# A spectral mixing layer beside an MLP on one core: another hand-written order of the first two weight blocks, a shorter normalisation factor, and another order of a product's passes

## The chip, the core and the metric

The kernel runs on one core of a Trainium2 chip. The metric is the device time of one execution in microseconds (us); the kernel before has three runs. Beside them stands one profiled execution, whose trace is read below.

## What is computed

```python
# x: 2048 x 576; w1: 576 x 4608; w2: 4608 x 576; the DFT matrices are 2048 x 2048 and 576 x 576, real and imaginary part
xn = _layernorm(x)                        # (x - mean) / sqrt(var + 1e-5)
a, b = xn @ dft_hid_re.T, xn @ dft_hid_im.T
y = dft_seq_re @ a - dft_seq_im @ b       # real part of a transform over both axes
h = maximum(xn @ w1, 0)
return x + y + h @ w2
```

## The kernel before

Every fp32 operand is split into a high and a low half in fp16 (the high part by ScalarE, the low part, the difference to it, by VectorE or GpSimd), and each product takes three passes on TensorE: high by high, high by low, low by high. The 4608 columns of the MLP are taken in nine blocks of 512 (b), the 2048 tokens in four groups of 512 (g), each of four tiles of 128 (t = 4 g + c). From block 1 on the products are made of seven sums of quarters in place of eight quarters (`PRODUCTS`, `pair_products`), whose operands are sums of quarters too. After the blocks come the two transforms.

All work stands in an order written out by hand: strings of words (`BLOCK0`, `BLOCK1`, `BLOCK` for each of blocks 2 to 7, `BLOCK8`, `TURN`). `run` and `run_block` go through the words and issue what each names; every engine does its own instructions in exactly that order, and waits at an instruction until its operands are there. The words that the prediction follows, with the lines of the profile:

- `f:n` issues n matmuls of nothing (`fill`, L1072), which keep TensorE going until there is work.
- `bn`, `ag`, `sq`, `ch` make mean, variance and the factor of a tile (L471, L475, L480, L487 to L492). `hi` writes the high half of the normalised tile (L511, L514), `xn` the normalised tile itself (L531 on ScalarE, L533 on VectorE), `lo` the low half (L519, L520, on VectorE where the word ends in V, on GpSimd where it ends in G).
- `T` transposes a tile's halves into `xT` by DMA from SyncE's queue (L541). For tiles 0 and 1 `th` and `tl` do it on TensorE instead (L552), and `ch_`, `cl` copy the result on ScalarE (L1111, L1112).
- `lx`, `L1`, `L2` load x, w1 and w2 (L344; L360, L371, L372; L348), also from SyncE's queue. `pa` to `pd` and `na` to `nd` make the scales of w1 of blocks 0 and 1, `q` and `rm`, `w` those of w2, from the sums of `sw` and `rw` (L960). `wh`, `wl`, `nh`, `nl` split w1 into halves (L918; L923, L924), `uh`, `ul` split w2 (L1013, L1017).
- `p:t:i` and `p0:f` are block 0's first product for a single tile (L586), `P:g:f` that for a group at once, `oa` and `od` its result's halves (L601, L609), `m:g:k` the second product (L847), `e` its eviction, `ad` the addition to `spill` in DRAM.
- `ts` makes sums of the normalised tiles (L653), `tu` and `tv` their halves (L511, L514; L519, L520), `tw` their transposes by DMA (L660, L664). There are two buffers for these halves (`spare`), used by turns, so a `tu` waits for the `tw` two places ahead of it to land.
- In block 1 `p:t:i:k` is one of the seven products (L710), `f:t:i:k` its way out of the bank (L700 on ScalarE, L702 on VectorE); a word that begins with 0 is one of block 0 that stands among block 1's.

A product's matmuls take the weight planes of `w1s` (0 to 2 high, 3 and 4 low, 2 holds both remainders) and those of `xT` in the order of `PASSES`; for the first products (`p0`) `WK0` puts the high planes first.

Of the kernel before, what the change touches and what calls it, by code (L numbers as in the profile page):

```python
# [78 lines left out]
p:0:0:1 w:0:1 p:0:0:5 p:0:1:1 0tu:3:3 0ad:2:1 0ad:1:3 0tv:3:3:G f:0:0:1:V w:0:2 w:0:3 0tu:3:2
f:0:0:5:A f:0:1:1:A p:0:0:6 p:0:1:6 w:0:4 f:0:0:6:A p:0:0:7 p:0:0:3 0tv:3:2:G 0e:2:3:V f:0:0:7  # L80
# [1522 lines left out]
```

## Time and profile before

| | us |
|---|---|
| three runs: median (lowest to highest) | 1232.77 (1230.32 to 1237.54) |
| the profiled execution: its own time | 1230.08 |
| its span from first to last instruction | 1228.3 |
| TensorE busy in it, pieces and waits included as the page counts them | 1216.8 |
| granted clock of TensorE, mean over the span | 1.00 of full speed |

The profiled execution lies 0.24 us below the fastest of the three runs and 2.69 us below their median. 1.8 us of its time lies outside its span. The page has the busy time of each engine; TensorE is busy for 99% of the span, and every other engine has idle time. So in this table the time of the kernel is TensorE's work and the few places at which TensorE stands still.

### The profile page before, as it was taken

What the parts mean: (1) busy time and instruction counts of PE and PEld (TensorE: products, weight loads), DVE (VectorE), ACT (ScalarE), POOL (GpSimd) and SP (SyncE); (2) the same over time, 40 slices, a digit from 0 to 9 for tenths busy, and PEclk for the clock granted to TensorE, in tenths of its full rate; (3) what the DMA queues carried; (4) which work ended last, traced back from release to release, by engine and by line L of the source; (5) the groups of instructions that cost most, each with busy time, mean ns of one, the idle gap of its engine ahead of it and who ended that gap; (6) DMA issues with size and microseconds to landing.
All of it is one profiled execution on the core that took longest, in us unless ns stands there. A gap on an engine that the chain in (4) does not pass through costs nothing.

```text
span 1228.3 us, 26251 instructions
## 1 busy us (share of the span) xinstructions
PE 1216.8 (99%) x10514; PEld 1000.4 (81%) x10514; DVE 1059.0 (86%) x2052; ACT 724.2 (59%) x1258; POOL 210.7 (17%) x272
## 2 busy tenths in 40 slices
PE   9999999999999999999999999998999999999998
PEld 9867888888888888888888888876777777777777
DVE  8977999989898889888888889999877869987885
ACT  7855776766756667657667547666444445534342
POOL 3522122122122121221121111200211110000000
PEclk9999999999999999999999999999999999999999
DMA  8997478778778777776666678631755532255441
GB/s 240 205 178 179 142 157 189 150 152 155 161 146 169 149 145 169 138 145 147 154 117 142 142 180 168 115 95 41 200 128 137 130 81 48 89 159 180 143 132 35
DMA packets 127052, 175.98 MB, mean 143 GB/s; under 512 B 48337, under 2 KB 88785, under 8 KB 126929
## 3 DMA queue, kind: packets, MB, share of 16 engines
q1 hardware_dynamic: 97696, 121.99, 34.1%
q0 software_dynamic: 28672, 51.92, 29.7%
q8 instruction: 82, 1.34, 0.5%
q10 hardware_dynamic: 560, 0.39, 0.1%
q14 instruction: 42, 0.34, 0.1%
HBM read 112.53 MB, written 56.62 MB: 138 GB/s over the span
## 4 chain that ended last, share of the span: by engine, by line
PE 90%; DVE 6%; DMA 2%; ACT 1%; issue 1%; POOL 1%; SPq 0%; DVEq 0%; POOLq 0%
PE bank L710 26%; PE p L1476 26%; PE p L807 25%; PE pd L1390 7%; PE p L586 3%; PE p L847 3%; DMA raw_w<-in_w_dram 1%; DVE R L1363 1%; DMA xT<-dbuf 1%; DVE st L471 0%; DMA accs<-in_x_dram 0%; DMA accs<-wbuf 0%; DVE wbuf L923 0%; DVE cs L1017 0%; DVE tb L1403 0%
## 5 line engine op out<-in xcount | busy, mean ns | idle before, releaser
L807 PE MATMUL p<-w2s,h 128*128 128x288 f16 x2688 | 357.3, 286 | 0.0
L1476 PE MATMUL p<-R,cs 128*128 128x288 f16 x2688 | 331.0, 286 | 2.5 <-DVE cs L1017 2.5
L1476 PEld LDWEIGHTS <-cs 128*128 128x128 f16 x2688 | 262.8, 98 | 69.6 <-DVE cs L1017 3.4
L807 PEld LDWEIGHTS <-h 128*128 128x128 f16 x2688 | 263.0, 98 | 62.1 <-issue 0.2
L710 PEld LDWEIGHTS <-dbuf 128*128 128x128 f16 x1568 | 153.2, 98 | 21.9 <-issue 1.9
L710 PEld LDWEIGHTS <-wbuf 128*128 128x128 f16 x1568 | 153.4, 98 | 20.6 <-issue 0.3
L1013 ACT ACTIVATE cs<-tb,sc_c 128x1024 f16<-128x1024 f32 x56 | 64.1, 1148 | 82.8 <-PE p L1476 55.7
L710 PE MATMUL bank<-xT,dbuf 128*128 128x256 f16 x896 | 110.9, 273 | 0.0
L710 PE MATMUL bank<-xT,wbuf 128*128 128x256 f16 x896 | 110.5, 273 | 0.1
L1017 DVE SCALAR_TENSOR_TENSOR cs<-tb,sc_c,cs 128x1024 f16<-128x1024 f32 x56 | 71.7, 1283 | 22.8 <-ACT cs L1013 22.2
L710 PE MATMUL bank<-accs,dbuf 128*128 128x256 f16 x672 | 86.3, 273 | 1.4 <-ACT accs L700 0.8
L832 POOL DMA_DIRECT2D spill<-dbuf x70 | 61.0, 912 | 155.3 <-DVE dbuf L825 112.4
L710 PE MATMUL bank<-accs,wbuf 128*128 128x256 f16 x672 | 85.9, 273 | 0.0
L1013 ACT ACTIVATE cs<-accs,sc_c 128x1024 f16<-128x1024 f32 x40 | 45.9, 1147 | 58.5 <-PE p L1476 45.7
L757 DVE TENSOR_TENSOR h<-s,h 128x1024 f16<-128x1024 f32 x64 | 77.4, 1217 | 2.4 <-ACT h L751 2.4
L751 ACT ACTIVATE h<-s 128x1024 f16<-128x1024 f32 x64 | 66.5, 1049 | 10.8 <-DVE s L748 10.8
L719 ACT ACTIVATE h<-accs 128x256 f16<-128x256 f32 x128 | 51.1, 410 | 33.0 <-DVE accs L734 23.7
L1237 ACT ACTIVATE f<-f 128x1024 f32<-128x1024 f32 x64 | 67.1, 1049 | 4.5 <-DMA f<-in_cim_dram 3.4
L832 POOL DMA_DIRECT2D spill<-wbuf x42 | 39.5, 940 | 155.0 <-DVE wbuf L825 126.5
L1017 DVE SCALAR_TENSOR_TENSOR cs<-accs,sc_c,cs 128x1024 f16<-128x1024 f32 x40 | 51.2, 1282 | 13.7 <-ACT cs L1013 13.3
L700 ACT ACTIVATE accs<-bank 128x256 f32<-128x256 f32 x99 | 37.4, 380 | 39.2 <-PE bank L710 13.6
L821 ACT ACTIVATE dbuf<-p,c_ub 128x576 f32<-128x576 f32 x61 | 45.0, 737 | 24.0 <-PE p L807 24.0
(227 smaller groups left out, 1898.5 us busy)
## 6 DMA issues: line engine op xcount, KB each, us to landing
spill<-dbuf POOLq DMA_DIRECT2D x80, 288.0 KB, 4.6
f<-in_cre_dram SPq DMA_DIRECT2D x32, 512.0 KB, 4.8
...
```

The lines of the kernel that those rows point to most:

```text
L710: nc.tensor.matmul(ps, l, r, start=first and m == 0, stop=m == len(todo) - 1, skip_group_check=not first,)
L719: nc.scalar.activation(next(high_low(q)), SOURCE[q], AF.Relu)
L751: order["s"] = nc.scalar.activation(next(high_low(SUMS)), stage_of(slice(1, 5)), AF.Copy).ins
L757: order["lo"] = nc.vector.tensor_tensor(lo, stage_of(slice(1, 5)), hi, ALU.subtract).ins
L807: nc.tensor.matmul(ps[:, c], h[:, x, qa, c * P : (c + 1) * P], w[:, y, qb], start=first and i == 0 and j == 0, stop=i == NQ - 1 and j == 2 ...
L821: freed(nc.scalar.activation(o, ps, AF.Copy, scale=us[b]))
L832: nc.gpsimd.dma_start(spill[g, row, col], sums[g, row, col], accum_op=ALU.add)
L1013: nc.scalar.activation(hi, src, AF.Copy, scale=s)
L1017: nc.vector.scalar_tensor_tensor(lo, src, s, hi, ALU.mult, ALU.subtract)
L1237: nc.scalar.activation(f, f, AF.Abs, scale=2.0**-10, accum_out=sums_c[:, n, q : q + 1])
L1390: nc.tensor.matmul(ps, x[:, k, c * P : (c + 1) * P], dsp[z][:, a, y], start=first and m == 0, stop=m == len(PASSES) - 1, skip_group_check= ...
L1476: nc.tensor.matmul(ps, w[:, a, RANK[k]], r[:, c, RIGHT[rq]], start=first and k == 0 and j == 0, stop=k == HK - 1 and j == 2, skip_group_ch ...
```

## The change

Three things are changed. The words of blocks 0 and 1 are put in another order, in which some are given to another engine; no word is added or taken away, but the number after `f` sums to 235 where it was 240. The factor of the normalisation takes five steps on VectorE where it took six: `sq` scales the root by 1/8, and one Newton step of the root and two reciprocals give the factor. And `WK`, the order of a product's 14 passes in block 0, has the high planes of both operands first, then the low planes of x, the remainders, and last the low planes of the weights, for `p0`, `p` and `P` alike.

```diff
 SX = 4.0
+CX = 0.5 / SX
 EPS = 1e-5
...
-    nc.vector.memset(eps, EPS)
+    nc.vector.memset(eps, EPS * CX * CX)
...
     def deviation(a, b):
-        nc.scalar.activation(u[:, a : b + 1], mv[:, a : b + 1, 1], AF.Sqrt, bias=eps)
+        nc.scalar.activation(u[:, a : b + 1], mv[:, a : b + 1, 1], AF.Sqrt, bias=eps, scale=CX * CX)
     def factor(a, b):
...
         nc.vector.reciprocal(r0[:, c], u[:, c])
-        stt(u[:, c], v, EPS, r0[:, c], ALU.add, ALU.mult)
-        tt(u[:, c], u[:, c], r0[:, c], ALU.mult)
-        nc.vector.tensor_scalar(u[:, c], u[:, c], -0.5 * SX, 1.5 * SX, ALU.mult, ALU.add)
-        tt(r[:, c], u[:, c], r0[:, c], ALU.mult)
+        stt(r[:, c], v, EPS, r0[:, c], ALU.add, ALU.mult)
+        stt(u[:, c], r[:, c], CX * CX, u[:, c], ALU.mult, ALU.add)
+        nc.vector.reciprocal(r[:, c], u[:, c])
         stt(sh[:, c], m, -1.0, r[:, c], ALU.mult, ALU.mult)
...
-    WK0 = sorted(WK, key=lambda w: (0, 0, 1, 2, 2)[w[1]])
+    WK.sort(key=lambda w: (w[2] > 2, w[2] > 2, 2, 3, 3)[w[1]])
+    WK0 = WK
...
 BLOCK0 = """
-bn:0 ag:0 sq:0:0 ch:0:0 bn:1 ag:1 bn:2 bn:3 ag:2 ag:3 ms:0 hi:0 sq:1:3 mc:0 f:121 pa:0 ch:1:3
+bn:0 ag:0 sq:0:0 ch:0:0 bn:1 ms:0 hi:0 xn:0:A ag:1 mc:0 bn:2 f:92 pa:0 f:9 th:0 ch_:0 bn:3 pb:0
...
```

Of the words that name an engine, those of blocks 0 and 1 together stand so: `xn` 11 on ScalarE and 5 on VectorE before, 14 and 2 now; `lo` 10 on GpSimd and 6 on VectorE before, 9 and 7 now; `ts` 6 and 10 before, 7 and 9 now; `tv` 6 and 10 before, 8 and 8 now; `e` 21 on ScalarE and 5 on VectorE before, 22 and 4 now; `f` 23 and 1 before, 22 and 2 now.

The lines of the changed kernel are two higher than those of before from the constants on, and one higher between the factor and the order of passes. What the new order does to the engines is seen at three places.

**The transposes of the third token group, on SyncE's queue, at about 43 to 54 us of the trace.** `raw_w1_1_0` and `raw_w1_1_1` are block 1's two halves of w1, `xT2` holds the third token group. Before:

```order
L660 DMA_TRANSPOSE accs_98<-wbuf_97 128x10x128
L360 DMA raw_w1_1_0_1227<-in_w1_dram 128x4x256
L371 DMA raw_w1_1_0_1227<-in_w1_dram 96x2x128
L372 DMA raw_w1_1_0_1227<-in_w1_dram 32x2x128
L371 DMA raw_w1_1_0_1227<-in_w1_dram 96x2x128
L372 DMA raw_w1_1_0_1227<-in_w1_dram 32x2x128
L541 DMA_TRANSPOSE xT2_136<-dbuf_96 128x10x128 x4
L664 DMA_TRANSPOSE accs_98<-wbuf_97 128x5x128
L664 DMA_TRANSPOSE xT0_134<-wbuf_97 128x5x128
L664 DMA_TRANSPOSE accs_98<-wbuf_97 128x5x128
```
Now:

```order
L346 DMA x14_100<-in_x_dram 128x576
L362 DMA raw_w1_1_1_1200<-in_w1_dram 128x4x256
L373 DMA raw_w1_1_1_1200<-in_w1_dram 96x2x128
L374 DMA raw_w1_1_1_1200<-in_w1_dram 32x2x128
L373 DMA raw_w1_1_1_1200<-in_w1_dram 96x2x128
L374 DMA raw_w1_1_1_1200<-in_w1_dram 32x2x128
L362 DMA raw_w1_1_0_1206<-in_w1_dram 128x4x256
L373 DMA raw_w1_1_0_1206<-in_w1_dram 96x2x128
L374 DMA raw_w1_1_0_1206<-in_w1_dram 32x2x128
L373 DMA raw_w1_1_0_1206<-in_w1_dram 96x2x128
L374 DMA raw_w1_1_0_1206<-in_w1_dram 32x2x128
L542 DMA_TRANSPOSE xT2_136<-dbuf_96 128x10x128 x4
```
Both loads of block 1's w1 now stand ahead of the four transposes into `xT2`; before, one of them stood ahead and the other behind the four transposes (L664) that follow.

**The first tiles on ScalarE, from 10.6 us on.** L480 is a root, L511 and L514 a high half, L531 a normalised tile, L918 a high half of weights, L1111 and L1112 the copies `ch_:0` and `cl:0`. Before:

```order
L480 ACTIVATE u_142<-mv_140,eps_138 128x3
L511 ACTIVATE dbuf_96<-accs_98,sh_144,r_143 128x2x256
L514 ACTIVATE dbuf_96<-accs_98,sh_144,r_143 128x2x2x32
L531 ACTIVATE accs_98<-accs_98,sh_144,r_143 128x576
L511 ACTIVATE dbuf_96<-accs_98,sh_144,r_143 128x2x256
L514 ACTIVATE dbuf_96<-accs_98,sh_144,r_143 128x2x2x32
L531 ACTIVATE accs_98<-accs_98,sh_144,r_143 128x576
L511 ACTIVATE dbuf_96<-accs_98,sh_144,r_143 128x2x256
L514 ACTIVATE dbuf_96<-accs_98,sh_144,r_143 128x2x2x32
L918 ACTIVATE wbuf_97<-raw_w1_0_0_148,c_sw1_210 128x2x384
L1111 ACTIVATE xT0_134<-p1_0_1_0_182 128x2x2x128
L1112 ACTIVATE xT0_134<-p1_0_1_1_183 128x2x3x128
```
Now (the copy `cl:0` is the row right behind these):

```order
L1113 ACTIVATE xT0_134<-p1_0_1_0_182 128x2x2x128
L482 ACTIVATE u_142<-mv_140,eps_138 128x3
L920 ACTIVATE wbuf_97<-raw_w1_0_0_148,c_sw1_200 128x2x384
L512 ACTIVATE dbuf_96<-accs_98,sh_144,r_143 128x2x256
L515 ACTIVATE dbuf_96<-accs_98,sh_144,r_143 128x2x2x32
L532 ACTIVATE accs_98<-accs_98,sh_144,r_143 128x576
L512 ACTIVATE dbuf_96<-accs_98,sh_144,r_143 128x2x256
L515 ACTIVATE dbuf_96<-accs_98,sh_144,r_143 128x2x2x32
L532 ACTIVATE accs_98<-accs_98,sh_144,r_143 128x576
L920 ACTIVATE wbuf_97<-raw_w1_0_0_148,c_sw1_200 128x2x384
L512 ACTIVATE dbuf_96<-accs_98,sh_144,r_143 128x2x256
L515 ACTIVATE dbuf_96<-accs_98,sh_144,r_143 128x2x2x32
```
The copy `ch_:0` and one of the weight halves have moved ahead of the three high halves of tiles 1 to 3.

**The end of block 0 on ScalarE, from about 102 us on.** `j` are the sums over w2 of block 1 (`rw`), `wbuf` from `x14` the last two `tu`, `accs` or `s` from a bank the first evictions of block 1's products. Before:

```order
L960 ACTIVATE j1_1_1795,c_mw2_1792<-raw_w2_1_1_1787 128x1152
L960 ACTIVATE j1_0_1797,c_mw2_1792<-raw_w2_1_0_1789 128x1152
L511 ACTIVATE wbuf_97<-x14_100 128x2x256
L514 ACTIVATE wbuf_97<-x14_100 128x2x2x32
L511 ACTIVATE wbuf_97<-x14_100 128x2x256
L514 ACTIVATE wbuf_97<-x14_100 128x2x2x32
L700 ACTIVATE accs_98<-bank3_1858 128x256
L700 ACTIVATE accs_98<-bank1_1856 128x256
L700 ACTIVATE s1_0_0_1925<-bank0_1855 128x256
```
Now:

```order
L860 ACTIVATE dbuf_96<-p2_0_2_0_1701,c_ub_896 128x576
L962 ACTIVATE j1_0_1797,c_mw2_1794<-raw_w2_1_0_1763 128x1152
L860 ACTIVATE wbuf_97<-p2_0_2_1_1769,c_ub_896 128x576
L962 ACTIVATE j1_1_1835,c_mw2_1794<-raw_w2_1_1_1765 128x1152
L512 ACTIVATE wbuf_97<-x14_100 128x2x256
L515 ACTIVATE wbuf_97<-x14_100 128x2x2x32
L512 ACTIVATE wbuf_97<-x14_100 128x2x256
L515 ACTIVATE wbuf_97<-x14_100 128x2x2x32
L702 ACTIVATE s1_0_0_1858<-bank0_1690 128x256
L702 ACTIVATE accs_98<-bank3_1693 128x256
```
Two evictions of block 0's second product (L860, before L858) now stand before and between the two sums, and one eviction of block 1's first product has gone ahead of this place (it stands five rows ahead of the first row shown, behind the last `oa`).

## Rows read from the trace of the kernel before

**Rows 1.** The page: busy time of each engine, share of the span, instructions

```profile
PE 1216.8 (99%) x10514; PEld 1000.4 (81%) x10514; DVE 1059.0 (86%) x2052; ACT 724.2 (59%) x1258; POOL 210.7 (17%) x272
```

**Rows 2.** Waits of TensorE before 230 us: total, times, longest

```profile
PE p L586 <- DMA xT<-dbuf: 1.5, 1, 1.5
...
PE bank L710 <- ACT accs L700: 0.8, 1, 0.8
PE bank L710 <- DVE s L736: 0.6, 1, 0.6
```

**Rows 3.** Timeline of TensorE: start us, us, line, tiles

```profile
19.38 0.49 PE L552 MATMUL p<-ident,dbuf 128*128 128x128 f16 x6
19.71 0.94 PE L586 MATMUL p<-xT,wbuf 128*128 128x128 f16 x14
...
21.08 10.38 PE L586 MATMUL p<-xT,wbuf 128*128 128x128 f16 x182 [0.21 <-DVE wbuf L923]
...
33.23 0.17 PE L441 MATMUL p<-row,ones 2*128 2x2 bf16 x1
...
45.85 11.92 PE L847 MATMUL p<-w2s,h 128*128 128x288 f16 x96
59.25 9.23 PE L586 MATMUL p<-xT,wbuf 128*128 128x512 f16 x42 [1.48 <-DMA xT<-dbuf]
...
108.70 0.22 PE L432 MATMUL bank<-ident,mb 128*2 128x128 bf16 x1
```

**Rows 4.** Timeline of ScalarE, start and end of block 0

```profile
18.06 0.57 ACT L1111 ACTIVATE xT<-p 128x512 f16<-128x512 f16 x1
18.54 0.79 ACT L1112 ACTIVATE xT<-p 128x768 f16<-128x768 f16 x1
...
105.65 1.16 ACT L960 ACTIVATE j<-raw_w 128x1152 f32<-128x1152 f32 x1 [2.08 <-DMA raw_w<-in_w_dram]
...
110.88 0.63 ACT L511 ACTIVATE wbuf<-x 128x512 f16<-128x512 f32 x1 [3.07 <-DVE half L444]
```

**Rows 5.** Timeline of VectorE, block 0

```profile
33.44 0.16 DVE L444 TENSOR_SCALAR half<-p 128x2 f32<-128x2 f32 x1 [0.39 <-PE p L441]
...
34.68 0.17 DVE L487 RECIPROCAL r<-u 128x4 f32<-128x4 f32 x1
...
35.75 0.22 DVE L519 TENSOR_TENSOR dbuf<-accs,dbuf 128x64 f16<-128x64 f32 x1
...
36.49 0.22 DVE L519 TENSOR_TENSOR wbuf<-first_xn,wbuf 128x64 f16<-128x64 f32 x1
...
38.46 3.22 DVE L1017 SCALAR_TENSOR_TENSOR w2s<-raw_w,c_sw,w2s 128x576 f16<-128x576 f32 x3
...
95.27 0.75 DVE L923 SCALAR_TENSOR_TENSOR dbuf<-raw_w,c_sw,dbuf 128x512 f16<-128x512 f32 x1
...
96.33 0.73 DVE L923 SCALAR_TENSOR_TENSOR dbuf<-raw_w,c_sw,dbuf 128x512 f16<-128x512 f32 x1
...
106.94 0.17 DVE L970 CAST mb<-c_mw 128x2 bf16<-128x2 f32 x1 [2.90 <-ACT j L960]
```

**Rows 6.** Timeline of SyncE's DMA queue

```profile
43.66 0.78 SPq L360 DMA_DIRECT2D raw_w<-in_w_dram  x1
...
46.67 7.72 SPq L541 DMA_TRANSPOSE xT<-dbuf  x4
...
98.29 2.29 SPq L348 DMA_DIRECT2D raw_w<-in_w_dram  x2
102.06 4.49 SPq L660 DMA_TRANSPOSE accs<-wbuf  x2
```

**Rows 7.** Chain that ended last, around 53 us

```profile
52.93 6.18 DMA xT<-dbuf
```

**Rows 8.** Timeline of GpSimd at 44 to 48 us

```profile
44.33 0.30 POOL L519 TENSOR_TENSOR dbuf<-accs,dbuf 128x64 f16<-128x64 f32 x1 [1.24 <-ACT accs L531]
...
46.33 1.43 POOL L519 TENSOR_TENSOR dbuf<-accs,dbuf 128x64 f16<-128x64 f32 x1 [0.57 <-DMA accs<-wbuf]
```

More of the change, by code (lines that the diff above doesn't have):

```diff
@@ L75 @@
-rw:0 e:2:1:V od:3:2 rm:0 tw:3:0 m:2:2 m:2:3
+bn:0 ag:0 sq:0:0 ch:0:0 bn:1 ms:0 hi:0 xn:0:A ag:1 mc:0 bn:2 f:92 pa:0 f:9 th:0 ch_:0 bn:3 pb:0
+pc:0 ag:2 ag:3 pd:0 sq:1:3 ch:1:3 mx:2 bn:4 bn:5 mx:3 wh:0 hi:3 xn:3:A hi:2 xn:2:A bn:6 bn:7
+lo:0:G lo:3:G lo:2:G wh:1 f:52 tl:0 f:38 pa:1 pb:1 hi:1 cl:0 lw:0 T:3 T:2 lx:8 f:24 pc:1 wl:1
+pd:1 ag:4 xn:1:A wh:2 f:13 p0:1 ag:7 ag:6 ag:5 wl:0 lo:1:V sq:4:7 wh:3 sw:0 th:1 f:7 p:3:0 tl:1
+lw:1 ch:4:7 hi:6 hi:4 wl:3 lx:11 xn:6:A cl:1 hi:5 wl:2 ts:0:0:V sw:1 p0:0 p:2:0 p:3:1 p:2:1
@@ new lines @@
+xn:4:V ch_:1 xn:5:A hi:7 lo:6:V ts:0:1:V lo:4:V bn:11 qm:0 ts:0:2:G p:0:1 p:1:1 qa:0 ts:0:3:V
+lx:10 lx:9 T:6 xn:7:A tu:0:1 bn:9 bn:8 qb:0 ag:8 ag:9 bn:10 oa:0:3 lo:5:G T:4 lo:7:G p:1:0 p:6:0
+qc:0 tu:0:0 ag:10 ag:11 qd:0 tv:0:0:V oa:0:0 uh:0:0 sq:8:11 uh:1:0 lx:13 tv:0:1:V ch:8:11 uh:1:1
+uh:0:1 oa:0:1 hi:8 oa:0:2 ul:1:1 ul:1:0 ul:0:0 ul:0:1 T:5 lx:12 T:7 lx:14 p:4:0 tw:0:0 p:6:1
+od:0:0 p:4:1 p:5:0 ts:1:0:G ts:1:1:G tw:0:1 lx:15 p:7:1 od:0:2 od:0:1 hi:10 xn:10:A xn:8:A p:5:1
+hi:11 od:0:3 bn:12 bn:13 bn:14 bn:15 tu:0:3 oa:1:3 xn:11:A hi:9 lo:10:G tu:0:2 m:0:0 xn:9:A
@@ new lines @@
+ag:12 p:7:0 ag:13 ag:15 oa:1:0 lo:8:G ag:14 ts:1:2:V sq:12:15 L1:1 L1:0 T:10 T:8 lo:11:V e:0:0:A
+tv:0:3:V lo:9:V ch:12:15 oa:1:2 oa:1:1 od:1:0 m:0:1 e:0:1:A od:1:3 m:0:2 ts:1:3:G hi:15 hi:12
+hi:13 xn:12:A tv:0:2:G nx:1 xn:15:V m:0:3 xn:13:A T:11 T:9 tw:0:3 lo:15:V ad:0:1 ad:0:0 tu:1:1
+hi:14 od:1:1 ts:2:0:G od:1:2 lo:12:V P:2:0 ts:2:1:V nx:0 P:2:1 tw:0:2 P:2:2 tv:1:1:G e:0:2:V
+oa:2:0 T:12 xn:14:A lo:13:G tu:1:0 oa:2:1 tw:1:1 tu:1:3 od:2:1 od:2:0 na:1 na:0 m:1:0 tv:1:0:G
+T:13 nb:0 lo:14:G tv:1:3:G tw:1:0 T:15 nc:0 nb:1 e:0:3:V oa:2:2 nc:1 m:1:1 od:2:2 nd:1 T:14
@@ L76 @@
+tu:1:2 nd:0 ad:0:3 ts:2:2:V ts:2:3:V ad:0:2 tv:1:2:V P:2:3 nh:1:0 nh:1:1 nh:0:1 nl:1:0 nh:0:0
+e:1:0:V oa:2:3 tw:1:3 tw:1:2 tu:2:1 e:1:1:A tu:2:0 ts:3:0:G nl:1:1 nl:0:1 ns:1:V tv:2:1:V P:3:0
+ad:1:0 tv:2:0:G nh:1:2 nl:0:0 od:2:3 ts:3:1:G tw:2:1 tw:2:0 tu:2:3 m:1:2 m:1:3 P:3:1 oa:3:0
+nh:1:3 oa:3:1 ns:0:V e:1:2:V tv:2:3:V P:3:2 ts:3:2:V od:3:0 P:3:3
 """
 BLOCK1 = """
[L79 to L80 removed]
@@ new lines @@
+w:0:2 w:0:3 p:0:1:6 w:0:4 p:0:0:7 p:0:0:3 p:0:0:2 f:0:1:6:V f:0:0:7 f:0:0:3 0ad:1:3 0ad:2:1
+0tv:3:3:G 0tv:3:2:G uh:0:0:0 0e:2:2:A uh:0:1:0 0tw:3:3 ul:0:0:0 0m:2:3 us:0:0 f:0:0:2 ul:0:1:0
+uh:0:0:2 0ad:2:0 0ad:2:2 0z:0 uh:0:0:1 p:0:1:5 p:0:1:2 0e:2:3:A p:0:1:7 p:0:0:4 m:-1:1 F:0:0
+ul:0:0:2 m:-1:0 h:0:0:11 0tw:3:2 r:0:0 h:0:0:12 S:0:0 ul:0:0:1 us:0:1 x:0:0 l:0:0:11 l:0:0:12
+uh:0:1:2 uh:0:1:1 h:0:0:22 L1:1:0 y:0:0 l:0:0:22 e:-1:1:A ul:0:1:2 ul:0:1:1 f:0:1:2 H:0:0
+f:0:1:5:A e:-1:0:A h:0:1:11 L1:1:1 p:1:0:1 p:0:1:3 f:0:1:7 h:0:1:22 f:1:0:1:A p:1:0:2 p:0:1:4
@@ new lines @@
+mx:1:0 h:0:1:12 f:0:1:3 L:0:0 mx:1:1 m:-1:2 r:0:1 x:0:1 l:0:1:22 p:1:0:5 0ad:2:3 y:0:1 R:1:0
+a:-1:0 a:-1:1 ph:1:0 mx:1:2 p:1:0:6 m:-1:3 nh:1:0:1 f:1:0:2 l:0:1:11 H:0:1 mx:1:3 f:1:0:5:A
+f:1:0:6:A e:-1:2:A F:0:1 h:1:0:11 L:0:1 l:0:1:12 e:-1:3:A R:1:1 ph:1:1 nh:1:1:0 p:1:0:7 p:1:0:3
+p:1:1:1 a:-1:2 nl:1:0:1 f:1:0:7 f:1:0:3 p:1:0:4 m:0:0 p:1:1:5 f:1:1:1:A nh:1:1:1 h:1:0:12
+h:1:0:22 r:1:0 nh:1:0:0 S:0:1 l:1:0:11 nl:1:1:0 l:1:0:12 l:1:0:22 a:-1:3 p:1:1:6 p:1:1:2
+nl:1:1:1 x:1:0 ns:1:1 f:1:1:6:A f:1:1:2 y:1:0 f:1:1:5:A m:0:1 p:1:1:3 p:1:1:7 p:2:0:1 p:2:0:2
@@ new lines @@
+f:1:1:3 e:0:0:A nh:1:1:3 f:1:1:7 e:0:1 h:1:1:11 f:2:0:1:A r:1:1 nh:1:1:2 h:1:1:22 p:1:1:4 m:0:3
+m:0:2 h:1:1:12 H:1:0 e:0:2:A F:1:0 S:1:0 e:0:3:A a:0:1 p:2:0:6 F:1:1 nl:1:0:0 x:1:1 ns:1:0
+l:1:1:22 y:1:1 f:2:0:2 nh:1:0:2 nh:1:0:3 L:1:0 p:2:0:5 m:0:4 l:1:1:12 e:0:4 H:1:1 f:2:0:5:A
+nl:1:0:2 a:0:4 m:0:5 f:2:0:6:A m:0:6 p:2:0:3 l:1:1:11 nl:1:0:3 nl:1:1:3 e:0:5 p:2:0:7 f:2:0:7
+nl:1:1:2 h:2:0:11 S:1:1 L2:1:0 F:2:0 L2:1:1 p:2:1:1 f:2:0:3 L:1:1 p:2:1:2 e:0:6:A f:2:1:1:A
+r:2:0 m:1:0 p:2:0:4 p:2:1:6 m:1:1 a:0:6 a:0:5 e:1:0:A h:2:0:22 h:2:0:12 sw:1:0 f:2:1:6:A p:2:1:5
@@ new lines @@
+p:2:1:7 f:2:1:2 x:2:0 l:2:0:22 h:2:1:11 y:2:0 e:1:1 f:2:1:5:A p:2:1:3 H:2:0 sw:1:1 m:1:3 p:3:0:2
+a:1:1 R:1:2 l:2:1:11 l:2:0:11 l:2:0:12 f:2:1:7 L:2:0 f:2:1:3 ph:1:2 S:2:0 r:2:1 h:2:1:22 p:3:0:1
+f:3:0:1:A m:1:2 p:3:0:6 p:3:0:5 p:2:1:4 uh:1:0:0 uh:1:1:0 l:2:1:22 f:3:0:2 f:3:0:6:A x:2:1
+ul:1:0:0 f:3:0:5:A e:1:2:A ul:1:1:0 F:2:1 h:2:1:12 e:1:3:A p:3:0:3 p:3:0:7 m:1:4 us:1:0 y:2:1
+f:3:0:3 e:1:4 S:2:1 uh:1:0:1 m:1:5 m:1:6 l:2:1:12 f:3:0:7 p:3:0:4 p:3:1:1 p:3:1:2 F:3:0 uh:1:0:2
+H:2:1 h:3:0:11 r:3:0 e:1:6:A ul:1:0:2 e:1:5 ul:1:0:1 L:2:1 f:3:1:1:A h:3:0:12 us:1:1 x:3:0
@@ L107 @@
+h:3:0:22 S:3:0 uh:1:1:1 f:3:1:2 l:3:0:22 y:3:0 l:3:0:12 ul:1:1:1 a:1:4 p:3:1:5 m:2:0 e:2:0:A
+uh:1:1:2 m:2:1 p:3:1:6 f:3:1:5:A f:3:1:6:A H:3:0 m:2:2 L1:2:0 h:3:1:11 p:3:1:3 a:1:5 F:3:1
+ul:1:1:2 p:3:1:7 e:2:1 e:2:2:A m:2:3 S:3:1 mx:2:0 mx:2:1 a:1:6 R:2:0 l:3:0:11 f:3:1:7 ph:2:0
+p:4:0:2 L1:2:1
 """
```

54 lines of the change are left out of this document (5 added, 49 removed).

## The prediction

> **What bounds the kernel now.** I read the page's busy times first: TensorE has something in it for 1216.8 us of the 1228.3 us span [rows 1]. So only two things can move the time: when its real work begins, and the places at which it stands still. The waits of TensorE come next. In the 230 us that hold blocks 0 and 1 it waits 1.5 us for a transpose into `xT`, and 0.8 and 0.6 us for evictions of block 1's first products [rows 2]; the other waits there lie ahead of the first product, or are 0.2 us. In TensorE's timeline the reader sees the same from the other side: small products without a pause from 21.08 us, 96 matmuls of the second product from 45.85, then the idle 1.48 us before `P:2:0` at 59.25 [rows 3]. The chain that ended last puts that wait on a transpose that was issued at 52.93 and took 6.18 us to land [rows 7].
>
> The matmul work is the same after the change, except for five fills of nothing, which stand where TensorE would wait for the same operands anyway: they cost nothing either way. This bounds the gain. If all three waits went (1.5 + 0.8 + 0.6) and the start came 0.5 us earlier (below), the kernel would win 3.4 us, 0.28%. About 0.5% (6.2 us) is what a measurement of this kernel can tell from no change. The loss has no such bound, so the rest looks for new waits.
>
> **The start.** Before, `p:3:0` began at 21.08, held for the last 0.2 us by a low half of weights [rows 3]. The new pass order takes low weights last, so that wait goes. On ScalarE the copy `ch_:0` (0.48 us, from 18.06 to 18.54) now stands in time that was idle, so `cl:0` can begin 0.48 us earlier than 18.54 [rows 4]. I put `p:3:0` at 20.25 in place of 21.08. But `tl:1`, six transposes of 0.33 us (19.38 to 19.71) [rows 3], now comes behind it: net 0.5 us earlier, at least 0 and at most 0.83. The factor's missing step is about 0.18 us (six from 34.68 to 35.75 [rows 5]), four times in block 0, beside other work.
>
> **The first place: `P:2:0`.** Does the early start survive the next wait? `P:2:0` needs all four transposes of group 2. Now ten issues of w1 stand ahead of them on SyncE's queue where five did. Step by step:
> - `qc` was at 33.23. One more small piece now stands ahead of it, 28 matmuls at 10.38/182 = 0.057 us, so 1.6; with `tl:1` and the earlier start it is at 33.23 + 1.6 + 0.33 - 0.83 = 34.3 [rows 3].
> - Behind it on VectorE: 0.2 us to begin, eight small steps (33.44 to 34.68, 1.24), two `tv` at 0.74 (35.75 to 36.49), the factor (1.07 less 0.18), four `ul` at 3.22/3 = 1.07 [rows 5]. That ends at 42.4. `L1:1` reuses the buffer that the last `ul` reads and can't be issued earlier.
> - A w1 half holds SyncE's queue for 43.66 to 46.67, 3.0 us [rows 6]. Two of them: 48.4, where the transposes began at 46.67. The last of the four was issued 6.26 us after the first (52.93 less 46.67) and took 6.18 to land [rows 6, 7]: 60.8, and `P:2:0` 1.6 us later than 59.25.
> From below: TensorE itself comes to `P:2:0` at 59.25 - 1.48 - 0.5 = 57.3, a gain of 2.0. Between the ends I take 0.8 later, nearer to the upper one, since each price on that side has a row; the `ul` and the landing can be a little cheaper. **Term: +0.8.** The early start is worth nothing here, as the queue, not TensorE, sets the time.
>
> The Trainium skill (DMA: Bandwidth & Descriptors, Issuing engines are not separate DMA queues) says that all DMAs end on the same 16 engines and interleave there, so the second w1 half's bytes would also lengthen the transposes' flight. No row here shows transposes behind two such loads; by the rule the term would be the upper end, +1.6, or above it.
>
> Behind `P:2:0` the queue has one w1 half less before group 3's transposes. `P:3:0` now comes before `m:1:2` and `m:1:3`, so TensorE asks one second-product group (11.92/4 = 2.98 us [rows 3]) earlier, and the queue is 3.0 us less loaded: no term.
>
> **The second place: the sums over w2 of block 1.** `L2` reuses the buffers of w1 of block 1 and so waits for the last `nl`. These now stand behind `nh:0:2` on ScalarE, and that behind the eviction `oa:3:2`.
> - From `P:2:0` to the first matmul of `w` (L432) were 108.70 - 59.25 = 49.45 us [rows 3]. `m:2:3` (2.98) has moved behind it and one product `p` (0.77, by columns from the 2.98) ahead: 47.2. With `P:2:0` at 60.05 it is asked for at 107.3.
> - `P:3:2` ends ahead of that by `P:3:3` (9.23/3 = 3.1), three `m` and two `p`: 13.6, so at 93.7. Then `oa` and `nh` (estimate 1.4 together), three `nl` at 1.06 (95.27 to 96.33) [rows 5]: `L2` at 98.3.
> - From the first issue of `L2` to the cast ahead of `w` were 98.29 to 106.94, 8.65 us, with the second sum waiting on ScalarE until 105.65 for its data [rows 4 to 6]: 106.95. No wait, with 0.3 us to spare.
> - But `tu:3:2` waits on ScalarE for a transpose that stands behind `L2` on the queue: 110.88 - 98.29 = 12.6 us after it [rows 4, 6]. 1.4 us of that may go, since those transposes, begun at 102.06 [rows 6], had themselves waited for GpSimd's half. So 109.5 to 110.9, and behind `tu:3:2` now stand the evictions that `p:0:0:7` needs, 1.1 us more. TensorE asks for it after `w` and three products, at 109.9: it waits 0.7 to 2.1 us, where it waited 0.8. Since both follow from the end of `P:3:2`, a late `P:2:0` changes nothing here. **Term: 0 to +1.3, taken as +0.7.**
>
> **Work that changes engine.** VectorE is rid of three `xn`, two `tv`, one `ts`, one `e` and gets one `lo` and one `f`; GpSimd gets two `tv` and a `ts` and loses a `lo`. The 0.6 us wait in block 1 [rows 2] may go or stay as VectorE runs ahead or not: **term -0.3**, ends -0.6 and 0. GpSimd's work is mostly hidden, but there is a price: the same small subtraction took 0.30 us at 44.33 and 1.43 at 46.33, while VectorE was at tensor-by-tensor work [rows 8]. The Trainium skill (SBUF — State Buffer, SBUF: two separate sides) calls the port pair of VectorE and GpSimd an exclusive lock, whole instructions long; the rows agree, and by it each moved `tv` or `ts` may cost its neighbour up to its own length.
>
> **Sum.** +0.8 + 0.7 - 0.3 = +1.2 us on the profiled execution's own 1230.08 us (1.8 outside its span): 1231.3. The four known times of the kernel before are 1230.08, 1230.32, 1232.77 and 1237.54, with their middle at 1231.5; a median of new runs should lie at that level, so I give 1232.7.
>
> **The rivals.**
> - *The waits go.* If `ul` ends early and the queue keeps ahead, `P:2:0` starts when TensorE comes (57.3), and the evictions are in time: -0.5 to -3.4 us, 1228 to 1231. For it: the new pass order, the early `ch_:0`, less VectorE work. Against: every step of the queue above has a row, and it has more in front, not less. 22%.
> - *The queue is worse than priced.* Transposes behind two loads of weights land 2 to 4 us later than 6.18, and `P:3:0` starts late too: +3 to +6 us, 1235 to 1238. For it: the landing was already 6.18 with one load ahead. 13%.
> - *`L2` late, and all of block 1 behind it.* `w`, `ul` of block 1 and all its second products follow `L2`. It decides from the point where `L2` is issued later than 98.6; each us later is a us for TensorE, since `w` stands in its line. Slower than 0.5% needs an issue after about 104, that is ScalarE held 5 us or more by `tu`s ahead of `nh:0:2`, each of which waits for a transpose: 1239 or more. 7%.
> - A win of more than 6.2 us has no place in the profile; 5% for a measurement that differs that much.
> - My forecast, within -0.5 to +3 us: 53%; its own range is 1231 to 1234.5.
>
> **How the numbers follow.** The range reaches to the low end of the waits that go (1231.5 less 3.4, and a little for runs that lie low) and to the high end of the worse queue (1231.5 plus 6): 1227.3 to 1237.8. Faster by over 0.5%: 5%; within 0.5%: 53 + 22 + 13 = 88%; slower: 7%.
>
> **What would show it.** In the trace after: `p:3:0` at about 20.3 without a wait for L923's successor; TensorE idle before `P:2:0` for 2 to 3.5 us, on a transpose, with the queue's four transposes beginning at 47.5 to 48.5; the first eviction-bound wait of block 1 at 109 to 112 us, 0.7 to 2.1 us long; nothing changed from 230 us on but the offset. I am wrong if the four transposes begin before 46.7, if `L2` is issued before 96 or after 100, or if TensorE shows a wait of over 2 us at a place that I don't name.

## The result and the profile after

Fourteen executions of each kernel: the changed one has a median of 1233.50 us (1230.35 to 1236.18), the kernel before 1230.43 us (1228.53 to 1237.54). The ratio is 1.0024, with a 95% interval of 1.0015 to 1.0034: slower by 3.0 us (1.8 to 4.2), where +1.2 was forecast. That is less than the 0.5% that the prediction took for what can be told from no change, but its interval leaves no change out. Two executions of the kernel before, beside the first experiments, took 3305 and 3918 us and stand in no comparison. The profiled execution of the changed kernel has a span of 1232.5 us, 4.2 more than the one before. Its busy times, from the page, answer to [rows 1]:

```profile
PE 1217.4 (99%) x10509; PEld 999.5 (81%) x10509; DVE 1059.1 (86%) x2040; ACT 726.6 (59%) x1261; POOL 211.5 (17%) x276
```

The waits of TensorE before 235 us, as in [rows 2]:

```profile
PE p L588 <- DVE dbuf L521: 2.7, 1, 2.7
PE bank L712 <- ACT accs L702: 1.1, 1, 1.1
...
PE p L809 <- DVE dbuf L827: 0.5, 1, 0.5
PE p L588 <- DMA xT<-dbuf: 0.4, 1, 0.4
```

TensorE's timeline, as in [rows 3]:

```profile
19.21 1.19 PE L588 MATMUL p<-xT,wbuf 128*128 128x128 f16 x14
...
21.37 1.72 PE L588 MATMUL p<-xT,wbuf 128*128 128x128 f16 x28 [0.36 <-DMA xT<-dbuf]
...
49.65 8.99 PE L849 MATMUL p<-w2s,h 128*128 128x288 f16 x72
61.38 10.91 PE L588 MATMUL p<-xT,wbuf 128*128 128x512 f16 x42 [2.73 <-DVE dbuf L521]
...
90.48 9.23 PE L588 MATMUL p<-xT,wbuf 128*128 128x512 f16 x42
...
109.98 0.22 PE L434 MATMUL bank<-ident,mb 128*2 128x128 bf16 x1
```

SyncE's queue, as in [rows 6]:

```profile
42.71 0.64 SPq L362 DMA_DIRECT2D raw_w<-in_w_dram  x1
...
45.58 0.61 SPq L362 DMA_DIRECT2D raw_w<-in_w_dram  x1
...
48.43 7.38 SPq L542 DMA_TRANSPOSE xT<-dbuf  x4
...
99.38 2.42 SPq L350 DMA_DIRECT2D raw_w<-in_w_dram  x2
```

and the four transposes by themselves (the queue's waits ahead of them and the time that each holds it, in ns, least, median and most, with the first and last start in us; then issue to landing in us):

```profile
L542 SPq EVENT_SEMAPHORE  x4: 17/28/28, 48.4 to 54.2; - x4
L542 SPq DMA_TRANSPOSE xT<-dbuf x4: 1307/1626/2516, 48.4 to 54.3; - x4
...
DMA to landing us min/median/max: 3.5/4.4/6.8
```

Two differences make nearly all of the 4.2 us. `P:2:0` begins at 61.38 in place of 59.25: 2.13 us. And the 42 matmuls behind that wait take 10.91 us in place of 9.23 [rows 3]: 1.68 us. The second has its reason in the granted clock, the column behind the busy time (with the instructions in brackets) in this table by stretches:

```profile
60.00:62.00 2.00, 0.62 (x3) 1.00 1.27 209
62.00:63.00 1.00, 1.00 (x5) 0.70 1.21 82
63.00:64.00 1.00, 1.00 (x4) 0.50 0.77 144
64.00:65.00 1.00, 1.00 (x3) 0.50 0.90 170
65.00:66.00 1.00, 1.00 (x4) 0.60 0.86 158
66.00:68.00 2.00, 2.00 (x11) 1.00 0.77 143
```

From 62 to 66 us TensorE has 0.50 to 0.70 of its clock. 0.50 is its lower level, 1.2 GHz in place of 2.4. In the profile of before the same stretch, behind an idle of 1.48 us, stayed at 1.00:

```profile
60.00:62.00 2.00, 2.00 (x11) 1.00 0.83 136
62.00:64.00 2.00, 2.00 (x11) 1.00 0.61 114
```

The rest is small: the waits behind block 0 are 1.1 + 0.5 us where they were 0.8 + 0.6. Together 2.13 + 1.68 + 0.2 = 4.0 of 4.2 us.

A warning on how waits are read: the page puts the 2.73 us on a subtraction of VectorE (L521). That one is a low half for the fourth token group, which `P:2:0` doesn't read; it ends at 61.35 by coincidence. The transpose issued at 54.28 that took 6.8 us landed at 61.1. In two of the experiments below the same wait is put on other steps of VectorE (L611, L534), in one rightly on the transpose.

### The profile page after: what moved, and what is told of

Its sections match the earlier page's. It is cut to its first block, busy times and chain, and to the rows that moved or that the text cites. A ratio compares the mean times of both kernels' runs of the same rounds, so it can differ in the third digit from the quotient of the medians.

```text
span 1232.5 us, 26234 instructions
## 1 busy us (share of the span) xinstructions
PE 1217.4 (99%) x10509; PEld 999.5 (81%) x10509; DVE 1059.1 (86%) x2040; ACT 726.6 (59%) x1261; POOL 211.5 (17%) x276
## 3 DMA queue, kind: packets, MB, share of 16 engines
q1 hardware_dynamic: 97696, 121.99, 34.3%
## 4 chain that ended last, share of the span: by engine, by line
PE 88%; DVE 4%; DMA 2%; issue 0%; ACT 0%; SPq 0%; POOL 0%; DVEq 0%; POOLq 0%
PE bank L712 26%; PE p L1478 26%; PE p L809 25%; PE pd L1392 7%; PE p L849 3%; PE p L588 2%; DMA raw_w<-in_w_dram 2%; DVE R L1365 1%; DVE dbuf L827 0%; DVE cs L1019 0%; DVE tb L1405 0%; DVE accs L1447 0%; DVE w2s L1019 0%; DVE wbuf L925 0%; DVE wbuf L926 0%
```

## The experiments

Theories. *Queue*: the second load ahead makes the transposes late. *Clock*: the idle before `P:2:0` also costs clock behind it. *Low half*: the last transpose waits for tile 9's low half, which ends late on VectorE in the new order. *Passes or factor*: the loss is not in the words at all.

**One load later.** In the new words:

```diff
-ag:12 p:7:0 ag:13 ag:15 oa:1:0 lo:8:G ag:14 ts:1:2:V sq:12:15 L1:1 L1:0 T:10 T:8 lo:11:V e:0:0:A
+ag:12 p:7:0 ag:13 ag:15 oa:1:0 lo:8:G ag:14 ts:1:2:V sq:12:15 L1:1 T:10 T:8 lo:11:V e:0:0:A
...
-hi:13 xn:12:A tv:0:2:G nx:1 xn:15:V m:0:3 xn:13:A T:11 T:9 tw:0:3 lo:15:V ad:0:1 ad:0:0 tu:1:1
+hi:13 xn:12:A tv:0:2:G nx:1 xn:15:V m:0:3 xn:13:A T:11 T:9 L1:0 tw:0:3 lo:15:V ad:0:1 ad:0:0 tu:1:1
```

> One half of block 1's w1 (its five issues) goes from ahead of the third group's four transposes to behind them; nothing else changes. Theory of the queue: the loads ahead make the transposes late. The four transposes begin at about 45.6 us in place of 48.43, the last of them still waits for its low half (VectorE, done at 54.0), but lands 4 to 5.2 us after its issue in place of 6.8; P:2:0 begins at 58.65 to 59.4 in place of 61.38, and with a wait below 1 us the granted clock stays at 1.00. The loss goes: ratio to the kernel before 0.9990 to 1.0003. Theory of the low half (VectorE's subtraction for tile 9, stretched by GpSimd, is what the last transpose waits for): issue at 54.1, landing as before, P:2:0 at 60.9 to 61.4, clock falls, ratio 1.0020 to 1.0026. Price that either must count: the first maxima of that half of w1 (61.99 on VectorE) may wait about 2 us for its data.

Measured: 1230.69 us, ratio to the kernel before 1.0000 (0.9990 to 1.0011). The loss against the kernel before is gone. TensorE's row, VectorE's low half of tile 9, and the queue's waits ahead of the transposes (ns, least, median and most):

```profile
58.19 9.22 PE L588 MATMUL p<-xT,wbuf 128*128 128x512 f16 x42
```

```profile
52.76 0.68 DVE L521 TENSOR_TENSOR dbuf<-accs,dbuf 128x512 f16<-128x512 f32 x1
```

```profile
L542 SPq EVENT_SEMAPHORE  x4: 17/502/1273, 45.5 to 52.2; - x4
L542 SPq DMA_TRANSPOSE xT<-dbuf x4: 1329/1613/1938, 45.8 to 53.5; - x4
```

Issue to landing of the last of the four alone:

```profile
DMA to landing us min/median/max: 4.6/4.6/4.6
```

`P:2:0` has no wait, and the clock stays. Once the queue is free, the low half is next in line: it ends at 53.44 and the last transpose goes at 53.5, behind a wait of the queue (1.27 us is the longest). In the changed kernel it ended at 54.01, 0.27 us ahead of an issue (54.28) that stood behind its three neighbours: the queue's waits there are 28 ns at most. So the queue set the time there, with the low half close behind. But the issue is the smaller part of what was won. The last transpose goes 0.8 us earlier (53.5 for 54.28) and is 2.2 us shorter in flight (4.6 for 6.8): it lands at 58.1, just as TensorE comes.

The ratio of 1.0000 hides one thing. None of these 12 executions has a mean granted clock that prints below 1.000, but 13 of the 34 of the kernel before beside them do. Against the other 21 of those (median 1229.65 us) this version is still 1.0 us longer.

**The low half first.** Both loads stay where the change put them; VectorE makes tile 9's low half before a low half of sums.

```diff
-tv:0:3:V lo:9:V ch:12:15 oa:1:2 oa:1:1 od:1:0 m:0:1 e:0:1:A od:1:3 m:0:2 ts:1:3:G hi:15 hi:12
+lo:9:V tv:0:3:V ch:12:15 oa:1:2 oa:1:1 od:1:0 m:0:1 e:0:1:A od:1:3 m:0:2 ts:1:3:G hi:15 hi:12
```

> On VectorE the low half of tile 9 goes ahead of a low half of sums (tv:0:3), so it is done at about 52.9 us in place of 54.0; both loads stay where the change put them. Theory of the queue: the last transpose is issued behind the three ahead of it at 54.2 to 54.3 all the same, P:2:0 begins at 61.2 to 61.5 and the clock falls: ratio to the kernel before 1.0020 to 1.0026. Theory of the low half: the last transpose goes up to 1 us earlier, P:2:0 begins at 60.3 to 60.6, ratio 1.0010 to 1.0017.

```profile
60.43 10.84 PE L588 MATMUL p<-xT,wbuf 128*128 128x512 f16 x42 [2.13 <-DVE h L611]
```

Measured: 1231.60 us, 1.0001 (0.9987 to 1.0015), which is lower than the theory of the queue alone allows. `P:2:0` came 0.95 us earlier than in the changed kernel and still waited 2.13 us, and the clock fell again (10.84 us). Of 12 executions 8 had a mean granted clock that prints below 1.000, against 12 of 14. The queue's waits ahead of the transposes:

```profile
L542 SPq EVENT_SEMAPHORE  x4: 17/28/28, 48.6 to 53.8; - x4
```

By its time the low half has a share, but no row shows it: the queue waited for nothing here, nor did it in the changed kernel, and the earlier start comes from transposes that held the queue and flew a little shorter. Profiles of one order differ by more than half a microsecond here (61.38 and, in the next experiment, 60.66), so the share isn't settled.

**Fills in the idle time.** 44 matmuls of nothing into `P:2:0`'s own bank.

```diff
         ps = ps1.tile([P, G], F32, tag="ps1", name=f"p1_{b}_{g}_{i}")
+        if (b, g, i) == (0, 2, 0):
+            for _ in range(44):
+                nc.tensor.matmul(ps[:, :P], ident, ident, start=True, stop=True)
         mlp1_group(b, g, i, slice(0, G), ps)
```

> 44 matmuls of nothing (0.057 us each, 2.5 us) into P:2:0's own bank, just ahead of its first pass, where TensorE stood idle for 2.73 us; all the rest is the changed kernel. Theory of the clock: the fall to half of the granted clock after 62 us follows from that idle time and costs 1.7 us, so with fills P:2:0 still begins its real passes at 61.2 to 61.5, but its 42 matmuls take 9.2 to 9.4 us in place of 10.91, the granted clock is 1.00 throughout, and the time is 1.4 to 1.8 us below the changed kernel: ratio to the kernel before 1.0008 to 1.0013. Rival: the clock falls for another reason (the load of the DMA engines at that place, or chance), the 42 matmuls take 10.5 us or more again and the ratio stays at 1.0020 to 1.0026.

```profile
57.89 2.62 PE L597 MATMUL p<-ident 128*128 128x128 f16 x44
60.66 9.23 PE L588 MATMUL p<-xT,wbuf 128*128 128x512 f16 x42
```

```profile
62.00:64.00 2.00, 2.00 (x11) 1.00 1.06 80
```

Measured: 1232.71 us, 1.0011 (0.9999 to 1.0023). The real passes begin at 60.66, still 1.4 us later than before, but they take 9.23 us for 42 with the clock at 1.00; 1 of 12 executions prints below 1.000, where 12 of 14 did. The theory of the clock holds. Its size in time is less sure: by the ratios (1.0024 and 1.0011 of 1230 us) 1.6 of the 3 us are clock, as in the profile (1.68), but the two intervals overlap.

**Both edits** (one load later and the low half first):

> Both edits: one load behind the transposes and the low half of tile 9 first. If queue and low half bound the last transpose together, it is issued at about 53 us, lands by 57.5 to 58.2, and P:2:0 begins when TensorE comes, at 58.65, without a wait: 3.8 to 4.4 us below the changed kernel, ratio to the kernel before 0.9988 to 0.9998. By the theory of the queue alone it is as with the load alone (0.9990 to 1.0003). If neither is the cause, ratio 1.0020 or more.

```profile
58.28 9.23 PE L588 MATMUL p<-xT,wbuf 128*128 128x512 f16 x42
...
170.10 2.45 PE L712 MATMUL bank<-accs,dbuf 128*128 128x256 f16 x21 [1.05 <-ACT accs L702]
```

Measured: 1229.42 us, 0.9989 (0.9979 to 0.9999). Run again beside the last experiment, on another chip:

> The version with one load later and the low half of tile 9 first, unedited, beside the one with the sum moved, on the same chip: ratio to the kernel before 0.9980 to 0.9998, as in its first run (0.9989, 0.9979 to 0.9999). If the kernel before happens to show few falls of the clock on this chip, the upper end.

1229.86 us, 0.9993 (0.9984 to 1.0002). It beats the changed kernel by some 4 us, and the kernel before by about 1, which is at the edge of what can be told. That 1 us is the clock of the kernel before: among executions that print 1.000 the medians are 1229.57 and 1229.77 us here, and 1229.65 and 1229.55 in the kernel before beside them.

**The words apart from the rest.** First the old words with the new factor and passes:

> The words of blocks 0 and 1 as before, the five-step factor and the new order of passes as in the change. If the words (the queue in front of P:2:0) are the whole loss, this stands at the kernel before: ratio 0.9988 to 1.0004, the idle before P:2:0 at 1.2 to 1.7 us, and the 0.21 us wait of p:3:0 for low weights gone. If the passes or the factor carry a part of the loss, ratio 1.0008 or more.

```profile
57.22 9.23 PE L587 MATMUL p<-xT,wbuf 128*128 128x512 f16 x42
```

1230.14 us, 0.9999 (0.9986 to 1.0012): nothing that can be told. The idle of 1.2 to 1.7 us that was expected in front of `P:2:0` isn't in this profile: the four transposes landed within 5.1 us there. Then the new words with the old factor and passes:

> The new words of blocks 0 and 1 with the six-step factor and the passes of before. If the words are the whole loss: idle before P:2:0 at 2.3 to 3 us, a lower granted clock behind it in most executions, ratio to the kernel before 1.0015 to 1.0034, as the change itself. If the passes or the factor carry it, ratio 1.0005 or less. A side effect that either must count: the first tiles of weights may wait 0.2 to 0.5 us for their low halves again.

```profile
60.79 9.22 PE L587 MATMUL p<-xT,wbuf 128*128 128x512 f16 x42 [2.22 <-DVE x L534]
```

1232.48 us, 1.0019 (1.0008 to 1.0029). The words are the loss, or nearly all of it: the interval of the run before leaves at most 0.12%, 1.5 us, for passes and factor. In this profile the clock happened to hold behind 2.22 us of idle; in 8 of the 12 executions its mean prints below 1.000.

**Fills in the kernel before** (the same edit with 25):

> The kernel before with 25 matmuls of nothing (1.4 us) ahead of P:2:0, in the 1.48 us in which its TensorE stood idle. In its own executions the mean granted clock was below 1.000 in 13 of 34, and these had a median of 1233.3 us against 1229.65 of the other 21. Theory of the clock (the idle in front of P:2:0 makes it fall, in the kernel before too, only less often): no execution with a mean granted clock under 0.9995, median 1229.2 to 1230.2, highest below 1232.5. Rival (those executions are slower for another reason, and the clock at that place is not what the idle does): 3 or more of 12 executions at 0.999 or below, and 1232 us or more in these.

1229.76 us, 0.9997 (0.9985 to 1.0008). The median came as expected, but one execution of 12 printed 0.999 and took 1235.36 us. On this chip the kernel before had only 6 such of 35, so 1 of 12 proves nothing: inconclusive.

**One load earlier, in the kernel before.** The one word of the change that the theory of the queue speaks of:

```diff
-oa:1:0 tu:0:2 tu:0:3 m:0:0 m:0:1 L1:0 T:11 T:8 oa:1:1 lo:10:G e:0:0:V bn:14 ag:13 ag:14 tv:0:2:G
+oa:1:0 tu:0:2 tu:0:3 m:0:0 m:0:1 L1:0 L1:1 T:11 T:8 oa:1:1 lo:10:G e:0:0:V bn:14 ag:13 ag:14 tv:0:2:G
...
-oa:2:2 lo:13:V tv:1:1:V tv:1:0:V lo:14:G L1:1 T:12 tw:1:1 od:1:3 nx:1 od:2:1 lo:15:G od:2:0
+oa:2:2 lo:13:V tv:1:1:V tv:1:0:V lo:14:G T:12 tw:1:1 od:1:3 nx:1 od:2:1 lo:15:G od:2:0
```

> The kernel before with one word moved: block 1's second half of w1 (five issues, 3.0 us of SyncE's queue) goes ahead of the third group's four transposes, as the change has it. Theory of the queue: the four begin at about 49.7 us in place of 46.67, the last is issued at about 56 and lands 6.2 to 6.8 later, P:2:0 begins at 62.2 to 63 where TensorE asks for it at 57.8; an idle of over 4 us, a fall of the granted clock in nearly every execution: 3 to 3.7 us for the start and 1.7 for the clock, ratio to the kernel before 1.0030 to 1.0045. Theory that the loads' place alone is harmless (the late low half of tile 9, which only the new order has, makes the loss): P:2:0 at 59 to 60, ratio below 1.0010.

Measured: 1235.78 us, 1.0044 (1.0030 to 1.0058); 9 of 9 executions print below 1.000. SyncE's queue, the chain that ended last, TensorE, and its clock by stretches:

```profile
49.92 7.86 SPq L541 DMA_TRANSPOSE xT<-dbuf  x4
```

```profile
54.74 7.57 DMA xT<-dbuf
```

```profile
62.56 10.80 PE L586 MATMUL p<-xT,wbuf 128*128 128x512 f16 x42 [4.84 <-DMA xT<-dbuf]
```

```profile
62.00:64.00 2.00, 1.44 (x4) 0.59 0.71 143
64.00:66.00 2.00, 2.00 (x6) 0.55 0.74 142
```

The transposes begin 3.25 us later than 46.67 [rows 6], TensorE starts 3.31 us later than 59.25 [rows 3], and the clock costs 1.57 more (10.80 less 9.23). Of the last transpose's delay, 1.81 us is its issue (54.74 for 52.93) and 1.39 its flight (7.57 for 6.18 [rows 7]). The queue alone, without the new order's late low half, is enough for a loss as large as the change's or larger.

**Two more waits taken away** from the version with both edits: `m:1:2` ahead of `P:3:0`, and an eviction, with its product, ahead of what stood before it on ScalarE.

```diff
-e:1:0:V oa:2:3 tw:1:3 tw:1:2 tu:2:1 e:1:1:A tu:2:0 ts:3:0:G nl:1:1 nl:0:1 ns:1:V tv:2:1:V P:3:0
-ad:1:0 tv:2:0:G nh:1:2 nl:0:0 od:2:3 ts:3:1:G tw:2:1 tw:2:0 tu:2:3 m:1:2 m:1:3 P:3:1 oa:3:0
+e:1:0:V oa:2:3 tw:1:3 tw:1:2 tu:2:1 e:1:1:A tu:2:0 ts:3:0:G nl:1:1 nl:0:1 ns:1:V tv:2:1:V m:1:2 P:3:0
+ad:1:0 tv:2:0:G nh:1:2 nl:0:0 od:2:3 ts:3:1:G tw:2:1 tw:2:0 tu:2:3 m:1:3 P:3:1 oa:3:0
...
-p:2:1:7 f:2:1:2 x:2:0 l:2:0:22 h:2:1:11 y:2:0 e:1:1 f:2:1:5:A p:2:1:3 H:2:0 sw:1:1 m:1:3 p:3:0:2
-a:1:1 R:1:2 l:2:1:11 l:2:0:11 l:2:0:12 f:2:1:7 L:2:0 f:2:1:3 ph:1:2 S:2:0 r:2:1 h:2:1:22 p:3:0:1
-f:3:0:1:A m:1:2 p:3:0:6 p:3:0:5 p:2:1:4 uh:1:0:0 uh:1:1:0 l:2:1:22 f:3:0:2 f:3:0:6:A x:2:1
+p:2:1:7 f:2:1:2 x:2:0 l:2:0:22 h:2:1:11 y:2:0 e:1:1 f:2:1:5:A p:2:1:3 H:2:0 sw:1:1 m:1:3 p:3:0:2 p:3:0:1 f:3:0:1:A
+a:1:1 R:1:2 l:2:1:11 l:2:0:11 l:2:0:12 f:2:1:7 L:2:0 f:2:1:3 ph:1:2 S:2:0 r:2:1 h:2:1:22
+m:1:2 p:3:0:6 p:3:0:5 p:2:1:4 uh:1:0:0 uh:1:1:0 l:2:1:22 f:3:0:2 f:3:0:6:A x:2:1
```

> The version with one load behind the transposes and the low half of tile 9 first, with two waits more taken away: the third group of the second product (m:1:2) goes ahead of P:3:0, which waited 0.6 us for a transpose, and an eviction on ScalarE (f:3:0:1) goes ahead of three pieces of work that stand behind a sum which waits for w2, where TensorE waited 1.05 us at 169 us. If TensorE's waits are the whole loss, each us of them is a us of time: 1.2 to 1.7 us below that version, 1227.7 to 1228.2, ratio to the kernel before 0.9970 to 0.9985. If other waits take their place (the evictions of P:3:0, now 3 us later), no gain: ratio 0.9985 to 0.9995.

The moved eviction writes over a buffer that a step of VectorE now reads only afterwards, so this kernel computes something else, and its time says only what its waits do. Its waits of TensorE from 160 to 175 us, and VectorE at that place:

```profile
PE bank L712 <- ACT accs L702: 2.0, 1, 2.0
PE bank L712 <- DVE s L738: 0.9, 1, 0.9
```

```profile
167.93 0.43 DVE L725 SCALAR_TENSOR_TENSOR h<-accs,h 128x256 f16<-128x256 f32 x1 [4.66 <-ACT accs L702]
```

1231.25 us, 1.0008 (1.0000 to 1.0017): no gain, and rather slower than without (0.9993, 0.9984 to 1.0002, on this chip). VectorE now waited 4.66 us for the eviction, and TensorE 2.9 us where it had waited 1.05. A miss.

**The sum later**, the mended form of that edit alone:

```diff
-a:1:1 R:1:2 l:2:1:11 l:2:0:11 l:2:0:12 f:2:1:7 L:2:0 f:2:1:3 ph:1:2 S:2:0 r:2:1 h:2:1:22 p:3:0:1
-f:3:0:1:A m:1:2 p:3:0:6 p:3:0:5 p:2:1:4 uh:1:0:0 uh:1:1:0 l:2:1:22 f:3:0:2 f:3:0:6:A x:2:1
+a:1:1 R:1:2 l:2:1:11 l:2:0:11 l:2:0:12 f:2:1:7 L:2:0 f:2:1:3 ph:1:2 r:2:1 h:2:1:22 p:3:0:1
+f:3:0:1:A S:2:0 m:1:2 p:3:0:6 p:3:0:5 p:2:1:4 uh:1:0:0 uh:1:1:0 l:2:1:22 f:3:0:2 f:3:0:6:A x:2:1
```

> The version with one load later and the low half of tile 9 first, with one sum of a transform's matrix (S:2:0, 1.25 us on ScalarE) put behind the eviction f:3:0:1, for which TensorE waited 1.05 us at 169 us. Expected: that wait shrinks to 0 to 0.3 us, 0.7 to 1.0 us below the unedited version beside it, if each us of TensorE's waits is a us of time. If another wait takes its place, no gain.

```profile
169.08 2.45 PE L712 MATMUL bank<-accs,dbuf 128*128 128x256 f16 x21
172.62 1.69 PE L712 MATMUL bank<-xT,dbuf 128*128 128x256 f16 x14 [1.09 <-ACT accs L702]
```

1229.46 us beside 1229.86 for the version without this edit; to the kernel before 0.9992 (0.9982 to 1.0002) beside 0.9993: no gain that can be told. The wait at 169 us went, and one of 1.09 us came three products later, behind two pieces of work on ScalarE that need the scale of w2. Both hang on one transfer of w2, and moving an eviction past one of its followers only hands the wait on.

## Why the prediction was wrong, step by step

**The step that failed** is the first place: "Between the ends I take 0.8 later, nearer to the upper one, since each price on that side has a row; the `ul` and the landing can be a little cheaper." and "Term: +0.8." The queue's steps came out right in their sum: the transposes began at 48.43 (said 48.4) and the last was issued at 54.28 (54.7). In their parts that was luck. `qc` came at 35.34, 1.0 later than the 34.3 worked out; the four `ul` took 3.0 us in place of 4.3; and the first load went at 42.71, before the last `ul` ended at 43.21, so it did not wait for that one. The landing was 6.8 us, not 6.18 or less, and `P:2:0` began 2.13 us later, above the upper end of 1.6. The lower end, a gain of 2.0, wasn't there to be averaged with: TensorE came at 58.65, not 57.3, so with every transpose in time the gain would have been 0.6.

**What was left out** is the larger half of the error in the profile. The idle itself was forecast (2 to 3.5 us; it was 2.73) and priced as if an idle microsecond cost a microsecond. Behind it the granted clock fell to 0.50, and the next 42 matmuls took 1.68 us more; the place cost 3.8 us in the profile where the term had 0.8. Fills in the idle time kept the clock at 1.00 and brought 1.6 us back by the ratios, whose intervals overlap. In the two of its 14 executions in which the mean granted clock printed 1.000 the changed kernel took 1231.63 and 1230.97 us; the kernel before had medians of 1229.5 to 1229.7 in its own. By these few, the loss without the clock is 1.3 to 2.1 us. The kernel with fills says more: in the 11 executions that print 1.000 it has a median of 1232.7 us, 3.0 above the kernel before on the same chip at 1.000. But its fills end at 60.5 us, and so hold `P:2:0` back wherever the transposes land sooner. How the 3.0 us of the medians divide between late start and clock stays open; the division into 2.13 and 1.68 is that of one profile.

The forecast of 1232.7 us lies only 0.8 below the measured 1233.50. That nearness is luck: the level it was added to, 1231.5, was 1.1 above the median of 1230.43 that the kernel before then showed, and the change itself was +3.0 in place of +1.2.

The Trainium skill (TensorE: Matmul & The Clock Gate, Part 1: The HAM clock gate) tells of a gate that passes half of the array's clock pulses when it has been little busy. The trace agrees: 0.50 from 63 to 65 us.

The rule on interleaved transfers that the prediction named (the Trainium skill, DMA: Bandwidth & Descriptors, Issuing engines are not separate DMA queues) pointed to the upper end or above, and so it came: 2.13 us for 1.6. In the five profiles with two loads of w1 ahead of the transposes the slowest of the four landed 5.6 to 7.6 us after its issue, in the eight with one load 4.7 to 6.2: later with more in front, though the two overlap.

**The start.** `p:3:0` was put at 20.25 and began at 21.37. The wait for low weights went, but the transpose of tile 3, issued at 16.55 and up to 4.8 us in flight, took its place (0.36 us). TensorE came to `P:2:0` 0.88 us later than before, not 0.5 earlier: `p:3:0` began 0.29 us later, the six transposes of `tl:1` (0.33) stood behind it, and a wait of 0.15 us for the first product's result came ahead of the second product. That cost nothing, as the prediction said of this place: the queue set the time.

**The second place.** `L2` was issued at 99.38 (between 96 and 100, as said), but the wait for evictions that was to grow to between 0.7 and 2.1 us was gone, 0.8 us won where the term had +0.7. The prediction's price from the end of `P:3:2` to `L2`, 4.6 us, was 2.9 (three products from 90.48 to 99.54, so the second ends at 96.5). Whether that is why the wait went wasn't tested. The third term had -0.3 and measured +1.0: the 0.6 us wait gave way to 1.1 and 0.5. The two together, +0.4 forecast and +0.2 measured, agree by luck.

**Work that changes engine.** The low halves show the price that was named: while GpSimd ran its own work, subtractions of 512 and 64 columns took 1.76 and 1.17 us on VectorE, where they otherwise take 0.68 (the last row below) and 0.22 [rows 5]. On VectorE and on GpSimd:

```profile
49.55 1.76 DVE L521 TENSOR_TENSOR dbuf<-accs,dbuf 128x512 f16<-128x512 f32 x1
...
52.23 1.17 DVE L520 TENSOR_TENSOR dbuf<-accs,dbuf 128x64 f16<-128x64 f32 x1
53.33 0.68 DVE L521 TENSOR_TENSOR dbuf<-accs,dbuf 128x512 f16<-128x512 f32 x1
```

```profile
49.45 2.05 POOL L655 TENSOR_TENSOR accs<-accs 128x512 f32<-128x512 f32 x2 [1.68 <-DVE accs L655]
...
51.72 1.60 POOL L521 TENSOR_TENSOR wbuf<-accs,wbuf 128x512 f16<-128x512 f32 x1
```

I had put this on the short side of work that is mostly hidden; it moved the low half of tile 9 to 54.01, 0.27 us from being the bound.

**The rivals.** "The queue is worse than priced" had the place and the sign, but not the way: the last transpose landed 0.6 us later than 6.18 and not 2 to 4, `P:3:0` had no wait, and the rest came from the clock.

**What stays open:** why the same order's transposes land half a microsecond or more apart from one execution to the next, the exact share of the low half, and how much of a transpose's longer flight behind two loads is their bytes and how much is chance.
